# A scan's block ends multiplied up in three levels instead of six steps, and both reciprocal roots of a unit issued together

## The chip, the cores and the metric

One NeuronCore of a Trainium2 chip runs the whole program. The metric is the device time of one execution in microseconds (us), the median of several runs. The engines are TensorE (PE; its weight loads are listed as PEld), VectorE (DVE), ScalarE (ACT), GpSimd (POOL) and SyncE (SP, which here only issues DMAs). Each engine executes its own list of instructions in order; an instruction that waits holds up everything behind it on its engine.

## The reference

The program is a gated linear attention with a complex decay, then a dense layer, then a mixture of experts:

```python
mag = np.sqrt(a_re * a_re + a_im * a_im)
scale = np.minimum(mag, 0.999) / (mag + 1e-06)
a_re_n, a_im_n = (a_re * scale, a_im * scale)
for t in range(S):                      # state D x D per head, complex
    S = a_n[t] * S + k[t] v[t]^T        # complex product, row by row
    y[t] = q[t] . Re(S)
x = y                                   # 3072 tokens x 384
h = x @ w_in;  x = (h * np.cos(h)) @ w_out        # 384 -> 2048 -> 384
e = argmax(x @ w_gate); out = gate * sigmoid(x @ w_output_gate)[e] * (relu(x @ w1[e]) @ w2[e])
```

Shapes: 4 batches x 8 heads x 768 steps x 48 channels; 8 experts of 384 -> 1024 -> 384.

## The kernel before, in words

The 768 steps of a batch are cut into chunks of 128; two chunks make a unit, so there are twelve units. Within a chunk the recurrence becomes matrix products once the running products of the decay are known. These running products are the scan, and it is done with channels on the partitions: `a_t` holds the decays of a unit (real part, imaginary part and a third plane), `l_t` the running products, `qk_t` the queries and keys.

For each unit the scan has these parts:

- `squares`: the squares of both parts on ACT (L227, L228) and their sum on DVE into `nt[:, 1]`.
- `root` (L235): ACT takes the reciprocal square root of that sum into the third plane of `a_t` (L237).
- `normal`: scales the decays; it reads what `root` left, first with an ACT square (L269).
- `core` (L291): 64 positions of half a chunk are stored as 8 blocks of 8. First the eight positions in each block are multiplied up (seven complex steps, L296 to L301, 192 elements each). Then come the block ends: the product over all earlier blocks is needed for each block. This is the stretch that the change rewrites (L305 to L330). `lb[:, :, :, 7]` is the last position of each block; `pb[..., i]` is to become the product of the ends of blocks 0 to i-1; `nb` holds signed copies of the imaginary parts (minus and plus), so that one multiplication gives both cross terms of a complex product. Six steps i = 2 to 7 each issue two multiplications and an addition of 24 elements per partition. Then four multiplications of 672 elements spread `pb` over the blocks, and one addition of 1344 elements writes `l_t`.
- `inverse` (L239): ACT squares `l_t` (L244), DVE adds, ACT takes the reciprocal root (L248) and squares it (L249), and DVE finishes 1/|l|^2 and multiplies it into `qk_t`. For units 2 to 10 it is also given the next unit (`ua`), and calls `root` for it right after L249 in program order.
- `post`: two DVE multiplications into `qkt`, and DMAs that turn heads onto partitions (`qkr`).

Then `attn` of the unit makes its 256 columns of `x` on PE, and the dense layer follows in eight slots per unit: `mm1` (18 matmuls, L509), `act2` on ACT (a square whose sum is kept L517, a sine L518, a square L519), `act3` on DVE (L548), which also frees the PSUM buffer `h` (two buffers), and `mm2` (8 matmul records, L564). The reciprocal root and the sine are in different activation tables of ACT, so going from the one to the other issues an `ACT_TABLE_LOAD`.

While the slots of unit u run, `attn` of u+1 and the scan of u+2 are interleaved with them. In the first units the weights `w_in` and `w_out` are also decoded on DVE (L693 to L696), checked on ACT (L704, L705), turned on PE (L738, into an `h` buffer or an `o` buffer), copied by ACT (L739), multiplied with the gate weights on PE (L741) and copied once more (L742). The experts run from about 720 us on.

What stands where in each engine's list is decided when the program is built: a scheduler plays the instructions against a cost table with priorities, and writes each engine's list in the order it found. So a changed instruction can move others, on every engine.

Of the kernel before, what the change touches and what calls it, by code (L numbers as in the profile page):

```python
# [10 lines left out]
F32 = mybir.dt.float32  # L11
# [4 lines left out]
AF = mybir.ActivationFunctionType  # L16
# [27 lines left out]
NCOL = 3 * UC  # L44
# [91 lines left out]
def build(tc, ap, out, force=False):  # L136
    nc = tc.nc
    V, A, G, PE, SY = nc.vector, nc.scalar, nc.gpsimd, nc.tensor, nc.sync
    ctx = ExitStack()

    def pool(name, bufs=1, **kw):
        return tc.tile_pool(name=name, bufs=bufs, **kw)
# [16 lines left out]
    sp = scan_ctx.enter_context(pool("sp", 1, side="left"))  # L159
# [27 lines left out]
    a_t = sp.tile([128, 3, NCOL, C], F32, name="a_t")  # L187
    qk_t = sp.tile([128, 2, NCOL, C], F32, name="qk_t")
    l_t = sp.tile([128, 2, NCOL, C], F32, name="l_t")
    nt = sp.tile([128, 2, NCOL, C], F32, name="nt")  # L190
    qkt = sp.tile([128, 2, NCOL, 2, QP], F32, name="qkt")
    t12 = sp.tile([128, 2, 2, NCOL * 16], F32, name="t12")
    nb = sp.tile([128, 2, 2 * NCOL, 8], F32, name="nb")
    pb = sp.tile([128, 2, 2 * NCOL, 8], F32, name="pb")
    m0 = sp.tile([128, 3, NCOL], F32, name="m0")
    one = sp.tile([128, 2, NCOL], F32, name="one")
# [7 lines left out]
    def tt(e, o, a, b, op):  # L204
        return e.tensor_tensor(out=o, in0=a, in1=b, op=op)  # L205

    mark = {}

    def behind(ins, *names):

        for n in names:
            tc.add_manual_dep(ins.ins, mark[n].ins.name,
                              mybir.DependencyInfo(mybir.DependencyClass.NoSync, mybir.DependencyReason.DATA),
                              reason="issue order")

    MUL, ADD, SUB = ALU.mult, ALU.add, ALU.subtract


    def load_a(u):
        SY.dma_start(a_t[:, 0:2], ap["a"][u])  # L220
# [4 lines left out]
    def squares(u):  # L225

        A.activation(out=a_t[:, 2], in_=a_t[:, 0], func=AF.Square)  # L227
        A.activation(out=nt[:, 1], in_=a_t[:, 1], func=AF.Square)  # L228
        yield
        tt(V, nt[:, 1], a_t[:, 2], nt[:, 1], ADD)  # L230
        yield

    rooted = set()

    def root(u):  # L235
        rooted.add(u)
        A.activation(out=a_t[:, 2], in_=nt[:, 1], func=AF.Abs_reciprocal_sqrt)  # L237

    def inverse(u, ua):  # L239

        sq = qflat[:, 0:2 * N1].rearrange("p (r c t) -> p r c t", r=2, c=NCOL)
        y, q = (qflat[:, N1 * i:N1 * (i + 1)].rearrange("p (c t) -> p c t", c=NCOL) for i in (2, 3))
        r = nt[:, 0]
        A.activation(out=sq, in_=l_t, func=AF.Square)  # L244
        yield
        mark["add", u] = tt(V, r, sq[:, 0], sq[:, 1], ADD)
        yield
        A.activation(out=y, in_=r, func=AF.Abs_reciprocal_sqrt)  # L248
        A.activation(out=q, in_=y, func=AF.Square)  # L249
        if ua is not None:  # L250
            root(ua)
        yield
        tt(V, r, r, q, MUL)
        yield
        V.scalar_tensor_tensor(out=r, in0=r, scalar=2.0, in1=q, op0=SUB, op1=MUL)
        V.tensor_reduce(out=chk[:, 2 * u + 1:2 * u + 2], in_=r[:, :, 63:128:64], op=ADD, axis=AX.XY)
        yield
        for qk in range(2):
            h = slice(64 * qk, 64 * qk + 64)
            o = qk_t[:, qk, :, h]  # L260
            V.scalar_tensor_tensor(out=o, in0=o, scalar=-1.0, in1=r[:, :, h], op0=MUL, op1=MUL)
        yield
# [25 lines left out]
    lb = l_t.rearrange("p r c (h j b) -> p r (c h) j b", h=2, j=8)  # L288
    ab = a_t.rearrange("p r c (h j b) -> p r (c h) j b", h=2, j=8)

    def core(u):  # L291
        n = 2 * NCOL
        for j in range(1, 8):
            t1, t2 = (t12[:, i].rearrange("p r (c b) -> p r c b", b=8) for i in range(2))
            pr = ab[:, 0:2, :, 0] if j == 1 else lb[:, :, :, j - 1]
            tt(V, t1, pr, ab[:, 0:1, :, j].to_broadcast([128, 2, n, 8]), MUL)  # L296
            tt(V, t2, pr[:, ::-1], ab[:, 2:0:-1, :, j], MUL)
            if j == 1:
                A.copy(lb[:, :, :, 0], ab[:, 0:2, :, 0])
            yield  # L300
            tt(V, lb[:, :, :, j], t1, t2, ADD)  # L301
            yield
        if u + 1 < NU:
            load_a(u + 1)
        V.tensor_scalar(out=nb[:, 0], in0=lb[:, 1, :, 7], scalar1=-1.0, scalar2=None, op0=MUL)  # L305
        V.tensor_copy(nb[:, 1], lb[:, 1, :, 7])
        V.tensor_copy(pb[:, :, :, 1], lb[:, :, :, 7, 0])
        yield
        for i in range(2, 8):
            t1, t2 = t12[:, 0, :, 0:n], t12[:, 1, :, 0:n]  # L310
            tt(V, t1, pb[:, :, :, i - 1], lb[:, 0:1, :, 7, i - 1].to_broadcast([128, 2, n]), MUL)
            tt(V, t2, pb[:, ::-1, :, i - 1], nb[:, :, :, i - 1], MUL)
            yield
            tt(V, pb[:, :, :, i], t1, t2, ADD)
            yield
        V.tensor_scalar(out=nb[:, 0, :, 1:8], in0=pb[:, 1, :, 1:8], scalar1=-1.0, scalar2=None, op0=MUL)
        V.tensor_copy(nb[:, 1, :, 1:8], pb[:, 1, :, 1:8])
        yield
        k = 2 * n * 56
        t1, t2 = (qflat[:, k * i:k * (i + 1)].rearrange("p (r c j b) -> p r c j b", r=2, c=n, j=8) for i in range(2))  # L320
        bc = [128, n, 8, 7]
        for r in range(2):
            tt(V, t1[:, r], lb[:, r, :, :, 1:8], pb[:, 0, :, 1:8].unsqueeze(2).to_broadcast(bc), MUL)
            yield
            tt(V, t2[:, r], lb[:, 1 - r, :, :, 1:8], nb[:, r, :, 1:8].unsqueeze(2).to_broadcast(bc), MUL)
            yield
        sq = squares(u + 1) if u + 1 < NU else iter(())
        next(sq, None)
        la = l_t.rearrange("p r c (h j b) -> p (r c h) j b", h=2, j=8)[..., 1:8]
        tt(V, la, t1.rearrange("p r c j b -> p (r c) j b"), t2.rearrange("p r c j b -> p (r c) j b"), ADD)  # L330
        yield
        gates(u)
        yield
        run(sq)
        yield
# [57 lines left out]
    def scan(u):  # L393
        if u == 0:
            yield from squares(u)
            yield from normal(u)
        yield from core(u)
        more = 1 < u < NU - 1
        yield from inverse(u, u + 1 if more else None)
        yield from post(u)  # L400
        if more:
            yield from normal(u + 1)
# [353 lines left out]
    def run(g):  # L756
        for _ in g:
            pass
# [491 lines left out]
    if True:  # L1250
# [29 lines left out]
        with tc.high_priority(offset=100):  # L1280
            run(core(1))
            run(inverse(1, None))
        with tc.high_priority(offset=100):
            run(post(1))
        for u in range(NU):
# [26 lines left out]
            for s in range(NS):  # L1312
# [6 lines left out]
                i = u * NS + s - 2  # L1319
# [56 lines left out]
```

## Time and profile before

| | us |
|---|---|
| median of 3 runs | 973.82 (973.53 to 974.1) |
| the profiled execution, its own time | 972.88 |
| its span, first to last instruction | 971.1 |
| PE busy in the span | 894.8 (92%) |
| PEld busy | 756.5 (78%) |
| DVE busy | 664.3 (68%) |
| ACT busy | 582.0 (60%) |
| POOL busy | 134.3 (14%) |

The span is the time between the first and the last instruction of one profiled execution; 1.8 us of its own time lie around it. Busy shares are means over stages that differ: the weights and the first two scans up to about 104 us, the first units of the dense layer up to 180 us, the steady interleaving up to 640 us, and the last unit and the experts after that.

### The profile page before, as it was taken

How to read it: one execution, taken by the hardware profiler on the slowest of the kernel's cores; microseconds unless marked ns; L12 is line 12 of the kernel's file. 1: busy time of each engine (PE TensorE's matmuls, PEld its weight loads, DVE VectorE, ACT ScalarE, POOL GpSimd, SP SyncE). 2: the span in 40 equal slices, each digit the busy share in tenths (PEclk: the TensorE clock that was granted, in tenths of full speed). 3: DMA queues.
4: the chain of work that ended last, by engine and by line, in shares of the span. 5: the costliest groups of instructions: out<-in, count | busy, mean ns of one | idle time of the engine just before them, and what ended most of it. 6: DMA issues, size and time to landing. Idle time of an engine off the chain costs nothing.

```text
span 971.1 us, 16175 instructions
## 1 busy us (share of the span) xinstructions
PE 894.8 (92%) x5701; PEld 756.5 (78%) x5701; DVE 664.3 (68%) x1498; ACT 582.0 (60%) x1252; POOL 134.3 (14%) x246
## 2 busy tenths in 40 slices
PE   0566897999999999999999999999999999999997
PEld 0455685877777787777777778789899899999997
DVE  6989885887779786979698788445664553355521
ACT  6684866757574848585757665365773453355521
POOL 0010001002123002020312121101121110312111
PEclk9999999999999999999999999999999999999999
DMA  9813046345333223232333231440328532554100
GB/s 328 313 43 106 20 114 207 100 120 167 102 85 122 66 95 85 90 95 90 89 101 85 97 96 47 115 142 22 106 76 259 167 128 66 175 182 140 25 28 33
DMA packets 69789, 109.93 MB, mean 113 GB/s; under 512 B 14063, under 2 KB 51327, under 8 KB 69428
## 3 DMA queue, kind: packets, MB, share of 16 engines
q1 hardware_dynamic: 62724, 98.72, 32.9%
q0 software_dynamic: 6976, 10.10, 3.1%
q8 instruction: 47, 0.77, 0.3%
q14 instruction: 42, 0.34, 0.1%
HBM read 74.20 MB, written 21.86 MB: 99 GB/s over the span
## 4 chain that ended last, share of the span: by engine, by line
PE 50%; DVE 19%; ACT 11%; DMA 8%; issue 6%; SPq 4%; POOL 0%; DVEq 0%; another core or an unknown queue 0%; ACTq 0%; POOLq 0%
PE o L564 12%; PE h L952 10%; PE h L509 10%; PE p L976 6%; PE p L968 4%; DVE t L205 3%; DVE qkt L205 2%; DMA a_t<-in_a_dram 2%; PE sc L438 2%; DVE l_t L205 1%; DVE g L548 1%; DMA xs<-in_xz_dram 1%; DVE pt L205 1%; PE m L473 1%; DVE nt L205 1%
## 5 line engine op out<-in xcount | busy, mean ns | idle before, releaser
L509 PE MATMUL h<-x,wi 128*128 128x256 f32 x1728 | 247.7, 294 | 14.9 <-DMA x<-x 5.6
L564 PE MATMUL o<-wo,g 128*128 128x400 f32 x672 | 246.2, 506 | 0.0
L509 PEld LDWEIGHTS h<-x,wi 128*128 128x128 f32 x1728 | 218.9, 191 | 34.4 <-issue 8.7
L564 PEld LDWEIGHTS o<-wo,g 128*128 128x128 f32 x672 | 121.2, 192 | 72.2 <-issue 4.4
L952 PE MATMUL h<-xe,w1t 128*128 128x384 f32 (+6 forms) x576 | 118.7, 349 | 0.0
L956 DVE SCALAR_TENSOR_TENSOR hh<-h,hh 128x384 fp32r<-128x384 f32 (+6 forms) x64 | 37.2, 582 | 117.5 <-ACT hh L955 116.9
L952 PEld LDWEIGHTS h<-xe,w1t 128*128 128x128 f32 x576 | 101.8, 188 | 5.2
L517 ACT ACTIVATE g<-h 128x512 f32<-128x512 f32 x96 | 57.1, 594 | 79.6 <-PE h L509 75.7
L955 ACT ACTIVATE hh<-h 128x384 fp32r<-128x384 f32 (+6 forms) x64 | 32.8, 514 | 114.1 <-PE h L952 107.5
L548 DVE SCALAR_TENSOR_TENSOR g<-g,h 128x512 f32<-128x512 f32 x96 | 65.5, 682 | 43.5 <-ACT g L519 42.3
L572 POOL DMA_INDIRECT xs<-rows,si x46 | 55.7, 1211 | 172.0 <-ACT x L466 41.0
L976 PE MATMUL p<-w2t,hh 128*128 128x384 f32 (+1 forms) x384 | 76.7, 343 | 0.0
L976 PEld LDWEIGHTS p<-w2t,hh 128*128 128x128 f32 (+1 forms) x384 | 66.0, 186 | 1.5 <-DVE hh L956 0.3
L519 ACT ACTIVATE g<-g 128x512 f32<-128x512 f32 x96 | 60.8, 633 | 1.8
L438 PEld LDWEIGHTS sc<-qkr 96*128 96x128 f32 x384 | 51.5, 203 | 11.7 <-issue 3.5
L438 PE MATMUL sc<-qkr 96*128 96x128 f32 x384 | 57.0, 293 | 3.8 <-DMA qkr<-qkt 2.4
L518 ACT ACTIVATE g<-h 128x512 f32<-128x512 f32 x96 | 57.6, 600 | 1.8
L205 POOL TENSOR_TENSOR fg<-l_t,m 128x12 f32<-128x12 f32 x24 | 4.7, 215 | 373.5 <-DVE l_t L205 241.8
L572 POOL DMA_INDIRECT out_dram<-o,tok x28 | 34.6, 1234 | 149.6 <-issue 57.4
L968 PE MATMUL p<-hh,w2t 128*128 128x448 f32 (+2 forms) x216 | 47.6, 359 | 0.0
L205 DVE TENSOR_TENSOR t<-l_t,a_t 128x192 f32<-128x192 f32 x144 | 45.0, 352 | 1.4
L205 DVE TENSOR_TENSOR qkt<-l_t,qk_t 128x1536 f32<-128x1536 f32 (+1 forms) x26 | 41.2, 1630 | 0.3
(299 smaller groups left out, 1501.7 us busy)
## 6 DMA issues: line engine op xcount, KB each, us to landing
stg<-in_w_dram SPq DMA_DIRECT2D x32, 768.0 KB
qkr<-qkt SPq DMA_DIRECT2D x96, 146.2 KB
a_t<-in_a_dram SPq DMA_DIRECT2D x12, 768.0 KB
qk_t<-in_qk_dram SPq DMA_DIRECT2D x12, 768.0 KB
xs<-in_xz_dram SPq DMA_DIRECT2D x17, 401.0 KB
raw<-in_w_in_dram SPq DMA_DIRECT2D x7, 768.0 KB
raw<-in_w_out_dram SPq DMA_DIRECT2D x7, 768.0 KB
vt<-in_v_dram SPq DMA_DIRECT2D x24, 192.0 KB
```

The source lines that it names most:

```text
L205: return e.tensor_tensor(out=o, in0=a, in1=b, op=op)
L438: PE.matmul(sc[:, h], lhsT=t[:, h, 1, 0:C], rhs=t[:, h, 0, 0:C], start=True, stop=True)
L509: PE.matmul(h[:, i], lhsT=wis[s][:, wi, kk, i * 128:(i + 1) * 128], rhs=x_t[u][:, xi, kk], start=n == 0, stop=n == 8)
L517: A.activation(out=g, in_=h, func=AF.Square, accum_out=hck[:, u * NS + s:u * NS + s + 1])
L518: mark["sin"] = A.activation(out=g, in_=h, func=AF.Sin, scale=0.5)
L519: A.activation(out=g, in_=g, func=AF.Square, scale=float(np.sqrt(2.0)))
L548: V.scalar_tensor_tensor(out=g, in0=g, scalar=1.0, in1=hps.pop((u, s)), op0=SUB, op1=MUL)
L564: PE.matmul(o, lhsT=a[:, i, cs], rhs=w[:, i], start=s == 0 and n == 0 and i == 0, stop=s == NS - 1 and n == len(prods) - 1 and i == 1)
L572: sc = G.indirect_dma_start(in_offset=None, oob_is_err=False, **kw)
L952: PE.matmul(h, lhsT=w[:, wi, kk, f * 128:(f + 1) * 128], rhs=x[:, xi, kk], start=n == 0, stop=n == 8)
L968: PE.matmul(o2[e][d][:, 0:c], lhsT=w[:, wi, f, d * 128:(d + 1) * 128], rhs=hh[:, hi], start=f == 0 and n == 0, stop=f == KE - 1 and n == 2)
L976: mm = PE.matmul(o2[e][j][0:w_, 0:DM], lhsT=hh[:, hi, j * w_:(j + 1) * w_], rhs=w[:, wi, f], start=f == 0 and n == 0, stop=f == KE - 1 and ...
```

## The change

Three things are edited. (1) The block ends are multiplied up in three levels (distance 1, 2, 4) on all blocks at once, the second and third in place in `pb`. Each level multiplies once by the real and once by the imaginary part of the other factor, and then subtracts for the real and adds for the imaginary part. (2) `nb` and its four copies go; the spreading multiplications read the imaginary part from `pb`, and the last addition becomes a subtraction for the real part and an addition for the imaginary part, of 672 elements each. (3) When `inverse` calls `root` for the next unit, `root` must stand behind the square L249 on ACT in issue order.

```diff
-    def root(u):
+    def root(u, *after):
         rooted.add(u)
-        A.activation(out=a_t[:, 2], in_=nt[:, 1], func=AF.Abs_reciprocal_sqrt)
+        behind(A.activation(out=a_t[:, 2], in_=nt[:, 1], func=AF.Abs_reciprocal_sqrt), *after)
...
-        A.activation(out=q, in_=y, func=AF.Square)
+        mark["rs"] = A.activation(out=q, in_=y, func=AF.Square)
         if ua is not None:
-            root(ua)
+            root(ua, "rs")
...
-        V.tensor_scalar(out=nb[:, 0], in0=lb[:, 1, :, 7], scalar1=-1.0, scalar2=None, op0=MUL)
-        V.tensor_copy(nb[:, 1], lb[:, 1, :, 7])
-        V.tensor_copy(pb[:, :, :, 1], lb[:, :, :, 7, 0])
-        yield
-        for i in range(2, 8):
-            t1, t2 = t12[:, 0, :, 0:n], t12[:, 1, :, 0:n]
-            tt(V, t1, pb[:, :, :, i - 1], lb[:, 0:1, :, 7, i - 1].to_broadcast([128, 2, n]), MUL)
-            tt(V, t2, pb[:, ::-1, :, i - 1], nb[:, :, :, i - 1], MUL)
-            yield
-            tt(V, pb[:, :, :, i], t1, t2, ADD)
-            yield
-        V.tensor_scalar(out=nb[:, 0, :, 1:8], in0=pb[:, 1, :, 1:8], scalar1=-1.0, scalar2=None, op0=MUL)
-        V.tensor_copy(nb[:, 1, :, 1:8], pb[:, 1, :, 1:8])
-        yield
+        last = lb[:, :, :, 7]
+        V.tensor_copy(pb[:, :, :, 1], last[..., 0])
+        for d, a, b in ((1, last[..., 1:7], last[..., 0:6]), (2, pb[..., 3:8], pb[..., 1:6]), (4, pb[..., 5:8], pb[..., 1:4])):
+            t1, t2 = (t12[:, i].rearrange("p r (c b) -> p r c b", b=8)[..., 0:7 - d] for i in range(2))
+            bc = [128, 2, n, 7 - d]
+            tt(V, t1, a, b[:, 0:1].to_broadcast(bc), MUL)
+            tt(V, t2, a, b[:, 1:2].to_broadcast(bc), MUL)
+            yield
+            tt(V, pb[:, 0, :, d + 1:8], t1[:, 0], t2[:, 1], SUB)
+            tt(V, pb[:, 1, :, d + 1:8], t1[:, 1], t2[:, 0], ADD)
+            yield
...
-            tt(V, t2[:, r], lb[:, 1 - r, :, :, 1:8], nb[:, r, :, 1:8].unsqueeze(2).to_broadcast(bc), MUL)
+            tt(V, t2[:, r], lb[:, 1 - r, :, :, 1:8], pb[:, 1, :, 1:8].unsqueeze(2).to_broadcast(bc), MUL)
...
-        tt(V, la, t1.rearrange("p r c j b -> p (r c) j b"), t2.rearrange("p r c j b -> p (r c) j b"), ADD)
+        for r, op in ((0, SUB), (1, ADD)):
+            tt(V, lb[:, r, :, :, 1:8], t1[:, r], t2[:, r], op)
```

The changed program is a few lines shorter, so its line numbers in what follows are smaller: L244 becomes L243, L248 L247, L249 L248, L237 L236, L517 to L519 L513 to L515, L726 L722, L739 L735 and L742 L738.

The first place is VectorE's list at the block ends of unit 2. The kernel before (the first three of six steps):

```order
L305 TENSOR_SCALAR nb_130<-l_t_126 128x96
L306 COPY nb_130<-l_t_126 128x96
L307 COPY pb_131<-l_t_126 128x24
L205 TENSOR_TENSOR t12_129<-pb_131,l_t_126 128x2x12
L205 TENSOR_TENSOR t12_129<-pb_131,nb_130 128x2x12
L205 TENSOR_TENSOR pb_131<-t12_129 128x24
L205 TENSOR_TENSOR t12_129<-pb_131,l_t_126 128x2x12
L205 TENSOR_TENSOR t12_129<-pb_131,nb_130 128x2x12
L205 TENSOR_TENSOR pb_131<-t12_129 128x24
```

The changed kernel, all levels and the first instructions behind them (`x` is a column block of the attention's output, `nt` the sum in `squares`):

```order
L305 COPY pb_130<-l_t_126 128x24
L204 TENSOR_TENSOR t12_129<-l_t_126 128x24x6 x2
L204 TENSOR_TENSOR pb_130<-t12_129 128x12x6 x2
L204 TENSOR_TENSOR t12_129<-pb_130 128x24x5 x2
L204 TENSOR_TENSOR pb_130<-t12_129 128x12x5 x2
L204 TENSOR_TENSOR x_732<-pv_t_136,x_732 128x4x128
L204 TENSOR_TENSOR t12_129<-pb_130 128x24x3 x2
L204 TENSOR_TENSOR pb_130<-t12_129 128x12x3 x2
L204 TENSOR_TENSOR qkt_128<-l_t_126,pb_130 128x672 x4
L204 TENSOR_TENSOR nt_127<-a_t_124,nt_127 128x768
L204 TENSOR_TENSOR l_t_126<-qkt_128 128x96x7 x2
```

Twenty-three small instructions have become thirteen larger ones, and the addition of 1344 elements two of 672.

The second place is ScalarE's list in the first unit, around its square of `l_t` (`raw` and `wo` belong to the decoding of the weights). Before:

```order
L742 COPY raw_173<-o1_585 128x16
L726 COPY wo_594<-raw_173 128x2x16
L227 ACTIVATE a_t_124<-a_t_124 128x768
L228 ACTIVATE nt_127<-a_t_124 128x768
L726 COPY wo_620<-raw_295 128x2x384
L739 COPY raw_295<-o0_602 128x384
L739 COPY raw_295<-o1_611 128x384
L244 ACTIVATE qkt_128<-l_t_126 128x1536
L237 ACTIVATE a_t_124<-nt_127 128x768
```

After:

```order
L226 ACTIVATE a_t_124<-a_t_124 128x768
L227 ACTIVATE nt_127<-a_t_124 128x768
L738 COPY raw_172<-o1_575 128x16
L243 ACTIVATE qkt_128<-l_t_126 128x1536
L735 COPY raw_285<-o0_592 128x384
L722 COPY wo_584<-raw_172 128x2x16
L735 COPY raw_285<-o1_601 128x384
L236 ACTIVATE a_t_124<-nt_127 128x768
L722 COPY wo_610<-raw_285 128x2x384
```

The square of `l_t` moved ahead of three copies of 384 and 768 elements and a small one, and L227 ahead of the copy that waits for PE.

The third place is ScalarE's list in the inverse of unit 2, between the last two copies of the weights' decoding; `h_1338` and `h_1310` are the first `mm1` buffer of unit 1. Before (a table load stands directly ahead of the first row):

```order
L237 ACTIVATE a_t_124<-nt_127 128x768
L742 COPY rawr_303<-h_1228 128x16
L726 COPY wo_1246<-rawr_303 128x16
L739 COPY rawr_304<-h_1237 128x384
L244 ACTIVATE qkt_128<-l_t_126 128x1536
L517 ACTIVATE g_1384,hck_118<-h_1338 128x512
L518 ACT_TABLE_LOAD
L518 ACTIVATE g_1384<-h_1338 128x512
L248 ACT_TABLE_LOAD
L248 ACTIVATE qkt_128<-nt_127 128x768
L519 ACTIVATE g_1384<-g_1384 128x512
L742 COPY rawr_304<-h_1237 128x16
```

After (ahead of the first row stand L243, a table load, L247 and the 16-column copy L738):

```order
L248 ACTIVATE qkt_128<-qkt_128 128x768
L236 ACTIVATE a_t_124<-nt_127 128x768
L722 COPY wo_1228<-rawr_293 128x16
L735 COPY rawr_294<-h_1219 128x384
L513 ACTIVATE g_1356,hck_118<-h_1310 128x512
L354 COPY qkt_128<-fg_135 128x24
L355 COPY qkt_128<-fg_135 128x24
L514 ACT_TABLE_LOAD
L514 ACTIVATE g_1356<-h_1310 128x512
L515 ACTIVATE g_1356<-g_1356 128x512
L268 ACTIVATE nt_127,chk_116<-a_t_124 128x768
L738 COPY rawr_294<-h_1219 128x16
```

The two roots now stand together behind one table load, and the copies of the weights' decoding moved behind them. Over the part of the list that is executed, the table loads go from 42 to 28.

## Rows read from the trace of the kernel before

**Rows 1.** Windows by stage: us, each engine's busy time (instructions), granted clock, DMA.

```profile
0.00:104.00 104.00, 50.38 (x250) 43.53 (x250) 88.70 (x183) 67.89 (x146) 3.18 (x17) 1.00 0.55 189
104.00:180.00 76.00, 68.67 (x430) 54.11 (x431) 57.65 (x109) 54.91 (x122) 5.84 (x26) 0.93 0.35 108
180.00:640.00 460.00, 450.99 (x3055) 352.66 (x3055) 359.55 (x834) 296.48 (x636) 75.42 (x153) 1.00 0.34 98
640.00:971.10 331.10, 324.78 (x1968) 306.17 (x1966) 158.41 (x374) 162.69 (x351) 49.86 (x50) 1.00 0.35 112
```

**Rows 2.** Waits of PE, 180 to 640 us: total us, times, longest.

```profile
PE sc L438 <- DMA qkr<-qkt: 2.2, 2, 1.4
PE pv_t L462 <- DVE tp L205: 1.6, 2, 1.3
PE h L509 <- DVE g L548: 1.3, 2, 0.7
```

**Rows 3.** DVE groups by shape: busy us, mean ns of one | idle before.

```profile
L205 DVE TENSOR_TENSOR t<-l_t,a_t 128x192 f32<-128x192 f32 x144 | 45.0, 352 | 1.4
...
L205 DVE TENSOR_TENSOR l_t<-qkt 128x1344 f32<-128x1344 f32 x12 | 18.6, 1550 | 0.0
```

**Rows 4.** Timeline of DVE, block ends of unit 1: start, us [idle before].

```profile
94.32 0.21 DVE L305 TENSOR_SCALAR nb<-l_t 128x96 f32<-128x96 f32 x1
...
97.71 0.20 DVE L205 TENSOR_TENSOR t<-pb,l_t 128x24 f32<-128x24 f32 x1
97.83 0.20 DVE L205 TENSOR_TENSOR t<-pb,nb 128x24 f32<-128x24 f32 x1
98.06 0.20 DVE L205 TENSOR_TENSOR pb<-t 128x24 f32<-128x24 f32 x1
...
98.53 1.62 DVE L205 TENSOR_TENSOR qkt<-l_t,pb 128x672 f32<-128x672 f32 x2
...
103.94 0.69 DVE L548 SCALAR_TENSOR_TENSOR g<-g,h 128x512 f32<-128x512 f32 x1 [1.38 <-ACT g L519]
```

**Rows 5.** Timeline of ACT, first unit, up to the square of l_t.

```profile
48.73 0.18 ACT L742 COPY raw<-o 128x16 f32<-128x16 f32 x1 [0.77 <-PE o L741]
...
50.54 0.87 ACT L726 COPY wo<-raw 128x768 f32<-128x768 f32 x1
51.32 0.87 ACT L739 COPY raw<-o 128x384 f32<-128x384 f32 x2
52.08 1.48 ACT L244 ACTIVATE qkt<-l_t 128x1536 f32<-128x1536 f32 x1
```

**Rows 6.** Timeline of DVE, first unit, the sum of those squares.

```profile
53.59 0.96 DVE L205 TENSOR_TENSOR nt<-qkt 128x768 f32<-128x768 f32 x1 [1.97 <-ACT qkt L244]
```

**Rows 7.** Timeline of PE, first transposes, and two later stalls.

```profile
63.64 0.90 PE L423 MATMUL m<-ident,qkt 128*128 128x128 f32 x3 [4.05 <-DVE qkt L205]
...
116.84 2.39 PE L509 MATMUL h<-x,wi 128*128 128x256 f32 x18 [0.66 <-DVE g L548]
...
170.25 4.74 PE L509 MATMUL h<-x,wi 128*128 128x256 f32 x25 [3.47 <-ACT rawr L742]
```

**Rows 8.** Timeline of DVE, 113 to 118 us: decoding of weights around one act3.

```profile
116.11 0.68 DVE L548 SCALAR_TENSOR_TENSOR g<-g,h 128x512 f32<-128x512 f32 x1
116.71 0.95 DVE L696 SCALAR_TENSOR_TENSOR raw<-raw 128x768 uint32<-128x768 uint32 x1
```

**Rows 9.** Timeline of ACT, inverse of unit 2.

```profile
158.66 1.28 ACT L237 ACT_TABLE_LOAD   x1
...
167.48 1.28 ACT L248 ACT_TABLE_LOAD   x1
168.77 0.84 ACT L248 ACTIVATE qkt<-nt 128x768 f32<-128x768 f32 x1
...
170.04 0.15 ACT L742 COPY rawr<-h 128x16 f32<-128x16 f32 x1
```

**Rows 10.** Window behind that stall: us, busy by engine, granted clock (third last).

```profile
170.20:173.00 2.80, 2.75 (x15) 2.75 (x16) 2.61 (x4) 0.83 (x2) 0.88 (x1) 0.61 0.01 3
```

More of the change, by code (lines that the diff above doesn't have):

```diff
@@ L192, in build @@
     t12 = sp.tile([128, 2, 2, NCOL * 16], F32, name="t12")
-    nb = sp.tile([128, 2, 2 * NCOL, 8], F32, name="nb")
     pb = sp.tile([128, 2, 2 * NCOL, 8], F32, name="pb")
@@ L328, in core @@
         next(sq, None)
-        la = l_t.rearrange("p r c (h j b) -> p (r c h) j b", h=2, j=8)[..., 1:8]
-        tt(V, la, t1.rearrange("p r c j b -> p (r c) j b"), t2.rearrange("p r c j b -> p (r c) j b"), ADD)
+        for r, op in ((0, SUB), (1, ADD)):
+            tt(V, lb[:, r, :, :, 1:8], t1[:, r], t2[:, r], op)
         yield
```

## The prediction

> **What bounds the kernel now.** I read the windows by stage first [rows 1]. Up to 104 us no engine is full, but DVE is busy for 88.7 us of it and ACT for 67.9, while PE works half the time: here the weights' decoding and the first two scans pass from engine to engine. From 104 to 180 us PE has 68.7 of 76.0 us. From 180 to 640 us PE is busy for 451.0 of 460.0 us, DVE for 359.6 (78%), ACT for 296.5 (64%). After 640 us PE has 324.8 of 331.1 us, and nothing that is changed runs there: the scan of the last unit is over. So the place decides what a saved microsecond is worth. In the head it may count in full. In the steady stage at most the 9.0 us in which PE is idle can come back, and the waits of PE say who owes them: the three largest are the DMA of the turned heads (2.2 us), DVE's `tp` (1.6) and `act3` (1.3) [rows 2]. All of these stand behind the scan's work in DVE's or ACT's list.
>
> A short stall costs PE more than its length. Behind the longest one after 104 us, 3.47 us long [rows 7], the granted clock is 0.61 over 2.8 us [rows 10], that is, mostly the lower level of 1.2 GHz, and the 25 matmuls there take 4.74 us [rows 7].
>
> **Part 1, the block ends.** In unit 1 they stand with nothing between them: from 94.32 to 98.53 us, so 4.21 us before the spreading begins [rows 4]. Two multiplications that don't depend on each other start 0.12 us apart, one that needs its predecessor 0.23 us behind it [rows 4]. The new shapes of 144, 120, 72, 60 and 36 elements aren't in the trace; they lie between 24 elements (0.20 us) [rows 4] and 192 (0.352 us) [rows 3], so about 0.9 ns for an element. A level is then two multiplications, a dependent subtraction and an addition. The first one costs 0.12 + 0.11 (120 elements more than 24, at 0.9 ns) for the first multiplication, 0.23 + 0.11 for the second, whose result is waited for, and 0.16 and 0.27 for the two of 72 elements: 1.00 us. In the same way 0.92 for the second and 0.79 for the third; with the one copy left, 0.1 to 0.2 us, it is about 2.85 us. The bounds are twelve instructions at 0.12 (1.4 us) and twelve at 0.352 (4.2 us). I take 2.85, as the sizes are nearer to 24 than to 192 in the last levels and in between in the first. The addition of 1344 elements (1.55 us) [rows 3] becomes two of 672, of which a pair of multiplications takes 1.62 us [rows 4]: 0.07 more. So DVE saves 4.21 - 2.85 - 0.07 = 1.3 us a unit, 15.5 us in all; by the bounds 0 to 2.7 us a unit.
>
> Next comes what is late instead. After the block ends of unit 1 DVE sits idle for 1.38 us until ACT's second square [rows 4]; in the first unit it waits 1.97 us for ACT's square of `l_t` [rows 6]. So in both, DVE's saving alone only lengthens a wait for ACT. I cost it at nothing there; ACT's own list is the cover, and where that list gets shorter, DVE's saving is what lets it be used. That the tile `nb` goes shifts other tiles in memory; no row shows that an address costs anything, so nothing for it.
>
> **Part 2, the head.** In ACT's list of the first unit the square of `l_t` now stands ahead of a copy of 768 elements and two of 384 (50.54 to 52.08 us, 1.5 us) and a small one (0.1), and L227 and L228 fill the 0.77 us in which ACT waited for PE [rows 5]. So ACT could start it at about 49.7 instead of 52.08. DVE writes `l_t` 1.3 us earlier, by about 48.5, and is no longer in the way. The copies that were passed over now stand between this square and the two of `inverse`, but DVE has six decode instructions of up to 0.95 us [rows 8] between its sum at 53.59 [rows 6] and the multiplication that needs them, which hides that. From there DVE is in one piece up to `post`, and PE's first transposes wait 4.05 us for it [rows 7]. I take -2.3 us, all on the path, since the DMAs of the turned heads and the first slot follow from it one by one. Bounds: 0 (the decoding of weights takes the time back) and -3.
>
> In the third slot of the first unit there is a small loss. DVE's list had one decode instruction behind an `act3` (116.71 behind 116.11) [rows 8], which now stands ahead of it; that `act3` is the one that PE waits for at 116.84, 0.66 us [rows 7]. One decode starts 0.87 us before its successor: +0.8.
>
> **Part 3, the roots.** Fourteen table loads fewer at 1.28 us [rows 9] are 18.0 us of ACT's time, of which 1.3 to 2.6 us fall in each unit from 2 on. The one PE stall that hangs directly on them is that of 3.47 us [rows 7]: PE waits for the last 16-column copy at 170.04, and on ACT this stands behind two table loads and both roots, 11.4 us after 158.66 [rows 9]. Before, three loads lie in that stretch (root, sine, root again); in the new list one lies in the shadow of DVE's sum and one in the open, so about two go (2.6 us). The square L268 comes into it (0.84, as L248 [rows 9]). It is shorter by about 1.7, but the copy still stands last, so I don't expect the stall to go: -1.2 us, between 0 and -5 (the stall and what the low clock costs behind it).
>
> The Trainium skill, "ScalarE: Activation LUTs", section What ACT_TABLE_LOAD costs, gives about 1283 ns for the load and 1380 ns more of drain, 2.66 us for a switch. The trace has the 1283 ns, but the next instruction starts 0.01 us behind the load's end (167.48 + 1.28, and 168.77) [rows 9], so no drain is seen. By the page fourteen loads would free 37 us of ACT; by the rows it is 18.0, and I use the rows.
>
> **Part 4, the steady stage.** There each of ten units frees 1.3 us on DVE and about 1.8 us on ACT, while PE waits 0.9 us a unit (9.0 in all). Most of these waits name an instruction that stood behind the scan's work, so more than half could go; but PE's list changes order too, and new waits come with it. I take -4.0, between 0 and -8.
>
> **Sum.** -2.3 + 0.8 - 1.2 - 4.0 = -6.7 us. The profiled execution took 972.88 us (span 971.1), so 966.2; the median of the runs shown stands 0.94 us above it, so 967.1.
>
> **Rivals.**
> 1. DVE, not PE, is the bound of the interleaved stages. For it: from 0 to 104 us DVE is the busiest engine [rows 1], PE's records are pipelined, so that a busy PE may be a slow one, and PEld is busy for only 352.7 of 460 us. Against it: DVE is idle for 100 us of the steady stage. It would give back the 1.3 us of twelve units, and 1 more in the first with its moved copies: 973.8 - 15.5 - 1 = 957. A rule of the Trainium skill, "Perfetto Trace Analysis", section Identifying the Most-Contended Engine, speaks for this rival: headroom of TensorE is to be read from the share of weight loads, not of matmuls, and that is 77% here against DVE's 78%. By that rule DVE would come first; the rows on PE's idle time name too little waiting for it.
> 2. Nothing comes through. PE is full in the steady stage, the head is paced by SP's DMAs and by the decoding, and what DVE and ACT save lengthens their waits. For it: both waits of DVE right after the block ends. Against it: PE's transposes do wait for DVE in the head. It gives 973.8, less 0 to 1.5: 973.
> 3. Slower. With the next unit's root behind the inverse, ACT runs load, L247, L248 and L236 as one block: 1.28 + 0.84 + 0.84 + 0.84 = 3.8 us, and waits in it for DVE's sum of 0.96 us. PE has two `h` buffers, and a slot of PE is 18 + 8 matmul records. From the point where this block, with that wait, outlasts a slot of about 5 us (2.39 us for the 18 [rows 7], and somewhat more for the 8), the next slot's squares come late in nine units. If each then costs a stall like the 0.66 us at 116.84 [rows 7], it is +5.9; with the +0.8 and half of the head that leaves +5.5: about 979. Against it: the block held two loads before, and the sine between them.
> 4. The change doesn't do what it says: if the scheduler parted the roots in most units, the loads would stay. ACT's list shows 28, so only one unit still has three loads; this rival is out, and gets no chance.
>
> **How the numbers follow.** My forecast has 0.62, with its own range of 962 to 971.5; rival 1 0.10, rival 2 0.17, rival 3 0.11. For this kernel 0.2%, some 2 us, is about what a measurement can tell from no change: faster below 971.9, slower above 975.8. Rivals 1 and most of the forecast are faster, 0.71; rival 2 and the rest 0.17; rival 3 0.12. The range reaches from 959.5 to 975, which leaves out rivals 1 and 3, 0.2 in all.
>
> **What would show it.** Right: DVE's block ends take 2.5 to 3.2 us; ACT's square of `l_t` in the first unit starts near 50, PE's first transposes near 61.5, and what follows them some 2 us earlier; table loads are 28; PE's idle time from 180 to 640 us is about 5 us. The stall at 170 is still there, near 2 us long. Wrong: PE's first transposes still at 63 us (then the head gave nothing), or PE idle as long as before in the steady stage with other names behind the waits (rival 2), or `mm1` waiting for `act3` in unit after unit (rival 3).

## The result, and the profile after

The changed kernel takes 965.0 us (median of 5 runs, 963.7 to 967.99) against 973.82 for the kernel before (5 runs, 972.28 to 974.1): a ratio of 0.9914, with a 95% interval of 0.9895 to 0.9933. The prediction was 967.1 us, with a range of 959.5 to 975. The profiled execution took 965.0 us, 963.2 of it span, against 972.88 and 971.1.

This window of the kernel after answers to the third row of [rows 1], with the same columns.

```profile
180.00:640.00 460.00, 455.94 (x3124) 359.55 (x3123) 354.14 (x757) 283.70 (x616) 68.84 (x153) 1.00 0.35 101
```

PE is idle for 460.0 - 455.9 = 4.1 us there, against 9.0, and gets 3124 matmul records done in it, against 3055. The waits of PE in that stage, which answer to [rows 2]:

```profile
PE sc L434 <- DMA qkr<-qkt: 2.1, 1, 2.1
PE pv_t L458 <- DVE tp L204: 1.4, 1, 1.4
PE pv_t L453 <- DVE pt L204: 0.6, 2, 0.3
```

These are nearly all that is left; the wait for `act3` is gone from the list.

VectorE's block ends of unit 1, which answer to [rows 4]:

```profile
92.75 0.19 DVE L305 COPY pb<-l_t 128x24 f32<-128x24 f32 x1
92.85 0.53 DVE L204 TENSOR_TENSOR t<-l_t 128x144 f32<-128x144 f32 x2
...
95.37 3.16 DVE L204 TENSOR_TENSOR qkt<-l_t,pb 128x672 f32<-128x672 f32 x4
99.60 0.96 DVE L204 TENSOR_TENSOR nt<-a_t,nt 128x768 f32<-128x768 f32 x1 [1.07 <-ACT nt L227]
```

They take 95.37 - 92.75 = 2.62 us, against 4.21. But the row at 99.60 shows VectorE idle behind the spreading, for ScalarE's second square of the next unit's decays. What those squares wait for is where the experiments end up.

Around unit 0 and unit 2 these rows answer to [rows 5], [rows 7] and [rows 9]. The timelines of ACT, DVE and PE (`raw` and `rawr` belong to the decoding of the weights):

```profile
50.12 1.51 ACT L243 ACTIVATE qkt<-l_t 128x1536 f32<-128x1536 f32 x1
...
153.70 0.84 ACT L226 ACTIVATE a_t<-a_t 128x768 f32<-128x768 f32 x1 [3.62 <-DMA a_t<-in_a_dram]
...
155.75 0.16 ACT L738 COPY raw<-h 128x16 f32<-128x16 f32 x1
...
168.72 0.15 ACT L738 COPY rawr<-h 128x16 f32<-128x16 f32 x1
```

```profile
81.97 0.68 DVE L204 TENSOR_TENSOR pt<-sc,cb 128x512 f32<-128x512 f32 x1
82.57 0.68 DVE L204 TENSOR_TENSOR x<-pv_t,x 128x512 fp32r<-128x512 f32 x1
```

```profile
61.97 0.90 PE L419 MATMUL m<-ident,qkt 128*128 128x128 f32 x3 [1.14 <-DVE qkt L204]
...
92.29 0.76 PE L505 MATMUL h<-x,wi 128*128 128x256 f32 x2 [5.29 <-DMA x<-x]
...
116.38 1.33 PE L505 MATMUL h<-x,wi 128*128 128x256 f32 x9 [1.39 <-DVE g L544]
...
155.97 0.92 PE L734 MATMUL h<-ident,rawr 128*128 128x128 f32 x3 [3.61 <-ACT raw L738]
...
168.93 3.58 PE L505 MATMUL h<-x,wi 128*128 128x256 f32 x18 [2.52 <-ACT rawr L738]
```

The square of `l_t` starts 2.0 us earlier, PE's first transposes 1.67 us, the first `mm1` only 0.93 us. The wait at 116 grew from 0.66 to 1.39 us, and the one at 169 shrank from 3.47 to 2.52. The wait at 156 grew too; in the kernel before it is this row of PE:

```profile
156.20 0.63 PE L738 MATMUL h<-ident,rawr 128*128 128x128 f32 x3 [2.20 <-ACT raw L742]
```

The copy that PE waits for there, at 155.75 on ScalarE, stands behind the square at 153.70, and that square waited 3.62 us for the load of the decays.

To compare kernels I use one stretch with the same work in each: from 104 us to the first evacuation of unit 9's output on ScalarE, in which every kernel has 3472 to 3488 matmul records on PE. Kernel before, then after (window, its length, busy time of PE; the rest of the row is not needed):

```profile
104.00:639.70 535.70, 519.36 (x3484) 406.60 (x3485) 416.90 (x943) 351.09 (x756) 81.26 (x179) 0.99 0.34 99
```

```profile
104.00:631.28 527.28, 515.65 (x3482) 406.10 (x3482) 407.42 (x851) 333.81 (x740) 72.35 (x169) 0.99 0.34 101
```

So unit 9 is evacuated 8.4 us earlier. PE's idle time falls from 16.3 to 11.6 us, and its busy time for the same work from 519.4 to 515.7: the gain is idle time and, nearly as much, faster matmuls.

### The profile page after: what moved, and what is told of

Same layout as the page of the kernel before. It is cut to its first block, busy times and chain, and to the rows that moved or that the text cites. A ratio compares the mean times of both kernels' runs of the same rounds, so it can differ in the third digit from the quotient of the medians.

```text
span 963.2 us, 16039 instructions
## 1 busy us (share of the span) xinstructions
PE 891.7 (93%) x5701; PEld 756.2 (79%) x5701; DVE 655.0 (68%) x1390; ACT 565.8 (59%) x1238; POOL 127.1 (13%) x246
## 4 chain that ended last, share of the span: by engine, by line
PE 66%; ACT 10%; DVE 8%; DMA 6%; issue 5%; SPq 4%; POOL 1%; DVEq 0%; ACTq 0%; POOLq 0%
PE o L560 19%; PE h L505 15%; PE h L948 10%; PE p L972 6%; PE p L964 4%; PE sc L434 3%; PE m L469 2%; PE pv_t L453 2%; DMA a_t<-in_a_dram 2%; PE pv_t L458 2%; SPq L365 1%; DVE t L204 1%; SPq L368 1%; DVE qkt L204 1%; DVE l_t L204 1%
## 5 line engine op out<-in xcount | busy, mean ns | idle before, releaser
L505 PE MATMUL h<-x,wi 128*128 128x256 f32 x1728 | 244.2, 293 | 13.4 <-DMA x<-x 6.2
L513 ACT ACTIVATE g<-h 128x512 f32<-128x512 f32 x96 | 57.2, 595 | 100.7 <-PE h L505 99.8
L568 POOL DMA_INDIRECT xs<-rows,si x46 | 51.3, 1114 | 249.6 <-ACT x L462 64.1
L515 ACT ACTIVATE g<-g 128x512 f32<-128x512 f32 x96 | 60.8, 634 | 2.0
```

The lines of the kernel that those rows point to most:

```text
L505: PE.matmul(h[:, i], lhsT=wis[s][:, wi, kk, i * 128:(i + 1) * 128], rhs=x_t[u][:, xi, kk], start=n == 0, stop=n == 8)
L513: A.activation(out=g, in_=h, func=AF.Square, accum_out=hck[:, u * NS + s:u * NS + s + 1])
L515: A.activation(out=g, in_=g, func=AF.Square, scale=float(np.sqrt(2.0)))
L568: sc = G.indirect_dma_start(in_offset=None, oob_is_err=False, **kw)
```

## Experiments

All runs with times. "Loads" are the table loads that ScalarE executes, "wait" is ScalarE's idle time in front of the first square of the next unit's decays (`a_t`) between 104 and 650 us, nine units in all; "idle" and "busy" are PE's in the stretch just told. These three are those of the profiled execution. The ratios are to runs of the kernel before on the same chip (medians 972.2 to 973.8 us).

| kernel | block ends | loads | time, us | ratio to before | wait | idle | busy |
|---|---|---|---|---|---|---|---|
| e4 | levels | 44 | 985.8 | 1.0143 [1.0122, 1.0164] | 33.9 | 24.6 | 521.1 |
| e12 (list of e1) | levels | 42 | 979.1 | 1.0061 [1.0041, 1.0080] | 36.5 | 25.4 | 518.9 |
| e1 | levels | 42 | 978.3 | 1.0058 [1.0038, 1.0078] | 32.4 | 18.9 | 518.4 |
| before | six steps | 42 | 973.8 | 1 | 25.7 | 16.3 | 519.4 |
| e5 | six steps | 38 | 967.1 | 0.9949 [0.9931, 0.9967] | 26.5 | 13.2 | 515.7 |
| e2 | six steps | 30 | 968.5 | 0.9965 [0.9947, 0.9983] | 20.0 | 12.7 | 518.5 |
| after | levels | 28 | 965.0 | 0.9914 [0.9895, 0.9933] | 32.1 | 11.6 | 515.7 |
| e11 (list of after) | levels | 28 | 964.0 | 0.9908 [0.9891, 0.9925] | 30.1 | 12.5 | 515.0 |
| e9 | six steps | 26 | 964.3 | 0.9906 [0.9887, 0.9926] | 26.3 | 11.1 | 516.1 |
| e8 | levels | 26 | 961.6 | 0.9872 [0.9849, 0.9894] | 34.1 | 9.6 | 514.7 |
| w9c | six steps | 26 | 958.7 | 0.9850 [0.9823, 0.9876] | 2.7 | 6.4 | 514.3 |
| w8b | levels | 26 | 958.3 | 0.9839 [0.9813, 0.9865] | 19.4 | 8.0 | 514.7 |
| w5c | levels | 28 | 954.4 | 0.9805 [0.9777, 0.9833] | 1.5 | 7.3 | 511.2 |
| w8c | levels | 28 | 954.1 | 0.9797 [0.9772, 0.9822] | 2.7 | 6.2 | 510.3 |

The profile puts most of this wait to the load (a DMA) and some of it to instructions of VectorE. In the kernel before, then after (total, times, longest):

```profile
ACT a_t L227 <- DMA a_t<-in_a_dram: 21.9, 7, 4.3
ACT a_t L227 <- DVE pb L205: 3.0, 1, 3.0
ACT a_t L227 <- DVE nb L316: 0.8, 1, 0.8
```

```profile
ACT a_t L226 <- DMA a_t<-in_a_dram: 27.5, 8, 5.8
ACT a_t L226 <- DVE mx L598: 4.6, 1, 4.6
```

The square needs nothing of `pb`, `nb` or `mx`. In the trace the last landing of the load stands at most 0.4 us ahead of the square's start in all of these waits, so they are one wait, and the column adds the lines up.

**The levels alone (e1).** The kernel after, without the hold on the root.

```diff
-            root(ua, "rs")
+            root(ua)
```

> The changed kernel with its three levels, but the next unit's root is not held behind the inverse: 42 executed table loads instead of 28, and lists on PE and DVE that hardly differ from the changed kernel's. Theory A (both parts free PE from waiting in the steady stage, the loads through ACT's list): about 3 us above the changed kernel, 967 to 970, with PE idle 6 to 8 us from 180 to 640 us. Theory B (VectorE's shorter list gives it all): 964 to 966. Theory C (the loads give it all): 972 to 974.

Measured: 978.3 us, slower than before. No theory had that. VectorE's work is shorter as in the kernel after, yet PE's idle time in the common stretch is 18.9 us, more than the kernel before has. The waits of PE from 180 to 650 us:

```profile
PE pv_t L453 <- DVE pt L204: 5.4, 3, 2.2
PE pv_t L458 <- DVE tp L204: 2.9, 2, 1.7
```

The longest of them, seen in the timeline of all engines (rows of the other instructions left out):

```profile
427.11 0.84 ACT L226 ACTIVATE a_t<-a_t 128x768 f32<-128x768 f32 x1 [3.50 <-DMA a_t<-in_a_dram]
427.86 0.83 ACT L227 ACTIVATE nt<-a_t 128x768 f32<-128x768 f32 x1
428.59 0.61 ACT L515 ACTIVATE g<-g 128x512 f32<-128x512 f32 x1
...
429.71 1.28 ACT L236 ACT_TABLE_LOAD   x1
...
432.93 1.28 ACT L514 ACT_TABLE_LOAD   x1
...
434.85 0.63 ACT L515 ACTIVATE g<-g 128x512 f32<-128x512 f32 x1
...
435.51 0.69 DVE L544 SCALAR_TENSOR_TENSOR g<-g,h 128x512 f32<-128x512 f32 x1 [1.56 <-ACT g L515]
...
436.59 0.68 DVE L204 TENSOR_TENSOR pt<-sc,cb 128x512 f32<-128x512 f32 x1
...
437.33 0.43 PE L453 MATMUL pv_t<-pt,vt 128*48 128x128 f32 x4 [2.20 <-DVE pt L204]
```

Read it from the end: PE waits for `pt`, which stands on VectorE behind `act3`; `act3` waits for ScalarE's square L515 at 434.85; and that square is late because ScalarE lost 3.50 us to the load of the decays and then 2 x 1.28 us to the table of the root, there and back. The square of the slot before, L515 at 428.59, had been queued behind L226 and L227 all that time.

**The roots alone (e2).** The six steps as before, the root held behind the inverse's square.

```diff
-            root(ua)
+            root(ua, "rs")
```

> The kernel before with its six steps and signed copies, but the next unit's root held behind the inverse: 30 executed table loads instead of 42, VectorE's work unchanged. Theory A: 969 to 972. Theory B: 973 to 975. Theory C: 964 to 967.

Measured: 968.5 us, a gain of 0.35%, on 30 loads. It lies just below the range of Theory A and above that of C. The parts don't add: levels +0.6%, roots -0.35%, both -0.9%. But this edit also moved other rows: some 960 of the 5701 in TensorE's list stand elsewhere than before, so it is not the roots' worth alone. Between e1 and the kernel after only some 180 do.

**Two repeats (e11, e12).** A further place for other work inside each level, with and without the hold.

```diff
             tt(V, t1, a, b[:, 0:1].to_broadcast(bc), MUL)
+            yield
             tt(V, t2, a, b[:, 1:2].to_broadcast(bc), MUL)
```

> The kernel after with one more place in each level of the block ends at which other work may be listed between the two products: same operations and the same 28 executed loads, other lists on all engines. Theory 1 (loads decide): 964 to 967. Theory 2 (order decides): off 965 by 2 us or more, 959 to 972.

> As the run e11_levels_other_order, without holding the reciprocal square root behind the inverse's square: 42 executed loads in place of 28. Theory 1: e11 + 14 x 1.28 = e11 + 18 us. Theory 2: within 5 us of e11 in either direction. Theory 3 (hidden until TensorE waits): e11 + 4 to 13, as the kernel with levels alone stood 13 us above the kernel after.

The scheduler put nothing there: the lists are, row for row, those of the kernel after and of e1. So both are repeats, not the other orders that I meant to test. As such they are useful: 964.0 beside 965.0, and 979.1 beside 978.3. The hold is worth 13 to 15 us where the block ends are levels, between what Theory 3 and Theory 1 said.

**The price of a table load (e4, e5, e9).** In e4 a sine of one element on ScalarE stands between the two roots, so that their tables are loaded apart again; the other lists differ from those of the kernel after in a dozen rows each at most.

```diff
+            mark["sn"] = behind(A.activation(out=spare, in_=one[:, 1, 0:1], func=AF.Sin), "rs")
-            root(ua, "rs")
+            root(ua, "sn")
```

> The changed kernel with a sine of one element between the square behind the first root and the second root of units 2 to 10, which adds two table loads of 1.28 us to most of these units (44 executed instead of 28, some 20 us of ScalarE) and leaves the lists of all other engines as they are, but for a few rows. Theory A: 3 to 5 us above the changed kernel, 968 to 970. Theory B: within 1 us of it, 964 to 966. Theory C: 972 or more.

Measured: 985.8 us, 20.8 more than after by the medians and 22.3 by the ratios, for 16 loads more (20.5 us at 1.28) and nine small sines: ScalarE's added time came through in full. That is inside Theory C's open range; A and B are out. The profiled executions differ by 18.0 us. In the common stretch it is 18.4, of which 13.0 are idle time of PE (24.6 against 11.6), and 5.4 slower matmuls (521.1 against 515.7).

In e5 three copies of the kernel before are written in the opposite order; e9 is e5 with the root held.

```diff
-        V.tensor_scalar(out=nb[:, 0], in0=lb[:, 1, :, 7], scalar1=-1.0, scalar2=None, op0=MUL)
-        V.tensor_copy(nb[:, 1], lb[:, 1, :, 7])
         V.tensor_copy(pb[:, :, :, 1], lb[:, :, :, 7, 0])
+        V.tensor_copy(nb[:, 1], lb[:, 1, :, 7])
+        V.tensor_scalar(out=nb[:, 0], in0=lb[:, 1, :, 7], scalar1=-1.0, scalar2=None, op0=MUL)
```

> The kernel before with its three copies at the block ends written in the opposite order: the same work to the instruction, but the scheduler's lists come out in another order on all engines. Theory A (the work that is saved counts): within 1.5 us of the kernel before, 972.3 to 975.3. Theory D (the order that the scheduler happens on makes the difference, and the gain is one draw of it): outside of that by 3 us or more, to either side.

> Block ends as before the change (six steps, signed copies, the three copies in the opposite order as in the run with 967.07 us), and the reciprocal square root of the next unit held behind the inverse's square: 26 executed table loads on ScalarE in place of 38, nearly the same lists of TensorE and VectorE otherwise. Theory 1 (a table load costs the kernel about its full 1.28 us): 967.1 - 12 x 1.28 = 951.7, cut off at about 956, since TensorE waits only some 12 us in all between 104 and 650 there. Theory 2 (the order of the lists decides, the loads are mostly hidden): 963 to 972 with no tie to the number of loads. Theory 3 (a load costs only while TensorE waits are left in the steady stage, which are 5.5 us there): 962 to 965.

e5 took 967.1 us, 0.5% less than before. That looked like the order alone, as Theory D has it, but its list also lost four table loads (38 for 42); how much is due to which was not separated. e9 took 964.3 us: twelve loads fewer than e5 gave only 2.8 us by the medians and 4.2 by the ratios, 0.2 to 0.35 us for each. So Theory 1 of that run (full price) is refuted for the six steps, and Theory 3 fits; Theory 2 could have this time too, but not the 15 us between e11 and e12, whose other lists are much alike. With the levels the same loads cost 1.0 us each (e1 and e12) to 1.4 us (e4). I read this as a matter of ScalarE's slack, of which more is gone with the levels; no run varies the slack alone.

**Where the slack went.** With 26 loads and six steps e9 takes the same time as the kernel after and its repeat with levels and 28 loads (964.3, and 965.0 and 964.0). There the levels' 1.5 us a unit on VectorE bring nothing. This led to Theory W: what VectorE saves comes out as ScalarE's wait for the decays. I took the figures for it from the lines that name the DMA, 27.5 us in the kernel after and 10 to 15 in e2 and e9. That was a misreading, since in those two more of the wait stands under other names. For e9:

```profile
ACT a_t L227 <- DMA a_t<-in_a_dram: 15.3, 5, 4.3
ACT a_t L227 <- DVE pb L205: 7.1, 2, 4.4
ACT a_t L227 <- DVE pt L205: 2.2, 1, 2.2
ACT a_t L227 <- DVE t L205: 1.7, 1, 1.7
```

Added up, it is 20.0 to 26.5 us in the four kernels with six steps and the squares where they were, and 30.1 to 36.5 in the six with levels. So the levels do lengthen the wait, but by 6 to 12 us, and most of it was there before.

The load of the next unit's decays overwrites `a_t`, so it can't start before the scan's last product has read it. In the kernel after, that pair of products starts at 417.94 on VectorE and the square at 423.01 on ScalarE, after a wait:

```profile
417.94 0.63 DVE L204 TENSOR_TENSOR t<-l_t,a_t 128x192 f32<-128x192 f32 x2
...
419.06 0.19 DVE L305 COPY pb<-l_t 128x24 f32<-128x24 f32 x1
...
423.01 0.85 ACT L226 ACTIVATE a_t<-a_t 128x768 f32<-128x768 f32 x1 [1.34 <-DMA a_t<-in_a_dram]
```

That is 423.01 - 418.57 = 4.4 us for the load. In other units SyncE issues it later, up to 7.0 us behind the product (unit 11), so its list adds to the wait. In units 2 to 9 the block ends, with what is listed among them, take 4.7 to 7.5 us with the six steps and 2.6 to 3.6 with the levels. The squares are written behind the spreading that follows; with the levels that comes sooner, and the rest of the load is waited for with the `act2` of the slots (their gates) queued behind. To test it, the squares are listed later.

**One wait of unit 2 taken out first (e8).** The squares of unit 2 go behind the first slot's gate (its `act2`), and its root behind the inverse's square.

```diff
+            root(u, *(["rs"] if u == 2 else []))
-        sq = squares(u + 1) if u + 1 < NU else iter(())
+        sq = squares(u + 1) if u + 1 < NU and u != 1 else iter(())
-                gs = chain((normal(2), scan(2)))
+                gs = chain((iter((None,)), squares(2, "g0"), normal(2), scan(2)))
```

> The kernel after, with unit 2's squares issued behind the first slot's gate and its reciprocal square root held behind the inverse's square: 26 executed loads in place of 28, and ScalarE no longer waits for unit 2's decays ahead of the first slot's gate. Theory 1: 965.0 - 2 x 1.28 - about 2 of TensorE's wait at 103.5 = 960.5 (959 to 962). Theory 2: anywhere within 5 us of 965, the wait at 103.5 gone or not. Theory 3: 962 to 964.

Measured: 961.6 us, 3.4 below the kernel after, inside the ranges of Theories 1 and 2 and 0.4 below that of Theory 3, so it doesn't part them. The wait of `mm1` for `act3` between 96 and 110 us fell from 3.2 to 2.2 us, but 2.2 us for a DMA of `x` came beside it. Unit 0 is evacuated at 167.8 us in place of 174.2, of which 3.0 us are left at unit 9, and the wait for the decays in the other units stayed (34.1 us).

**The squares late (w5c), and the same with the six steps (w9c).** Only the issue order of two ScalarE instructions in units 3 to 11 is asked for, and the work is the same, but the scheduler's other lists change with it: some 900 of TensorE's 5701 rows stand elsewhere in w5c than in the kernel after, and some 630 in w9c than in e9.

```diff
         for r, op in ((0, SUB), (1, ADD)):
-            tt(V, lb[:, r, :, :, 1:8], t1[:, r], t2[:, r], op)
+            mark["la"] = tt(V, lb[:, r, :, :, 1:8], t1[:, r], t2[:, r], op)
+        if 1 < u < NU - 1:
+            behind(mark["s0", u + 1], "la")
+            behind(mark["s1", u + 1], "la")
```

> The kernel after, with ScalarE's two squares of the next unit's decays listed behind the last sum of the scan (VectorE) in place of ahead of it: same work, 28 executed loads as in the kernel after. Theory W (what the levels save on VectorE came out as ScalarE's wait for the load of the decays, 27.5 us between 104 and 650 in the kernel after, 10 to 15 us in the kernels with the six steps and the roots in one trip): that wait falls under 10 us, and the time to 959 to 963. Rival S (that wait is slack of ScalarE and costs nothing): 963 to 967, whatever the wait.

> The kernel of the run with 964.25 us (six steps, copies in the opposite order, roots in one trip, 26 executed loads) with the same late squares, still 26 loads. Theory W: there is less of the wait to remove (15.3 us), so less is won: 962 to 965, and the kernel with the levels and late squares is at least 1.5 us faster. Rival S: 962 to 967 and within 1.5 us of it.

Measured: 954.4 us for w5c, 10.6 below the kernel after, and 958.7 for w9c, 5.6 below e9. Both are better than Theory W's own ranges, and outside those of Rival S. In w5c this is left of the 32.1 us of ScalarE's wait:

```profile
ACT a_t L226 <- DVE qkt L204: 1.1, 2, 0.7
ACT a_t L226 <- DMA a_t<-in_a_dram: 0.4, 1, 0.4
```

The common stretch of w5c:

```profile
104.00:622.44 518.44, 511.18 (x3484) 402.21 (x3485) 405.95 (x851) 332.34 (x741) 85.45 (x172) 1.00 0.35 102
```

Against the kernel before w5c saves 17.3 us in this stretch, 9.1 of idle time and 8.2 of busy time. And with the wait gone the levels are worth something: w5c is 4.3 us below w9c, although it has two loads more.

Where this is won says more than the sum. From 104 us to the first evacuation of unit 0, the kernel after, then w5c:

```profile
104.00:174.15 70.15, 62.58 (x403) 50.02 (x403) 54.51 (x97) 49.97 (x116) 3.51 (x16) 0.93 0.40 122
```

```profile
104.00:168.09 64.09, 59.46 (x413) 47.72 (x414) 50.88 (x94) 49.04 (x114) 4.65 (x19) 1.00 0.39 122
```

Of the 8.8 us by which w5c is ahead of the kernel after at unit 9, 6.1 are won here, where only one of the nine waits lies, that of 3.62 us at 153.70. In w5c the copy that PE waits for stands ahead of the squares, and the squares don't wait. The timelines of ACT and PE:

```profile
152.82 0.17 ACT L743 COPY raw<-h 128x16 f32<-128x16 f32 x1
...
155.34 0.85 ACT L226 ACTIVATE a_t<-a_t 128x768 f32<-128x768 f32 x1
```

```profile
153.04 0.63 PE L739 MATMUL h<-ident,rawr 128*128 128x128 f32 x3 [0.32 <-ACT raw L743]
```

PE waits 0.32 us there and not 3.61. Two stalls of 0.76 and 0.54 us, at 158 and 163, come in place of that of 2.52 us at 169, and the granted clock of the stretch is 1.00 and not 0.93. The other eight waits, 28.5 us of them, lie behind, and what lies between the evacuations of units 0 and 9 is shorter by only 2.8 us. In w9c, too, 4.2 of the 6.5 us at unit 9 are won before unit 0's evacuation, but in part by a stall at 118 that lies ahead of all late squares (2.30 us in e9, 0.75 in w9c), so by the order of the lists.

**Both together (w8c, w8b).** The late squares in e8, once behind the last sum as in w5c, once one sum earlier.

```diff
-            behind(mark["s0", u + 1], "la")
-            behind(mark["s1", u + 1], "la")
+            behind(mark["s0", u + 1], "sp")
+            behind(mark["s1", u + 1], "sp")
```

> The kernel of the run with 961.59 us (no wait of ScalarE for unit 2's decays ahead of the first gate) with the late squares: 28 executed loads in place of 26. Theory W: 956 to 960. Rival S: 961 to 964, since two loads come back and nothing is won.

> As w8c_no_wait_unit2_late, but the squares behind the last spreading product, one sum earlier: 26 executed loads. Theory W: between 957 and 961, with a wait for the decays between that of the kernel before it (30.7 us) and that of w8c. Rival S: 961 to 963.

Measured: 954.1 us for w8c, below Theory W's range, and 958.3 for w8b, inside it. With e8 that makes three sizes of the wait: 34.1 us and 961.6, 19.4 us and 958.3, 2.7 us and 954.1, on average 0.24 us for each microsecond of ScalarE's wait (7.5 us for 31.4). From e8 to w8b only some 55 rows of TensorE's list change, from e8 to w8c some 440. It is an average and not a price, as the places where w5c won its time show. w8c is not distinguishable from w5c; no gain of the edit for unit 2 is to be seen once the squares are late. Both stand some 2% below the kernel before (the intervals reach from 1.7 to 2.3%).

## Why the prediction was right, step by step

| step | predicted, us | measured, us |
|---|---|---|
| block ends of a unit | 2.85 | 2.62 |
| head, at the first `mm1` | -2.3 | -0.9 |
| third slot, decode ahead of `act3` | +0.8 | +0.7 |
| stall at 170 | -1.2 | -0.95 |
| right behind that stall, up to unit 0's evacuation | 0 | -1.3 |
| steady stage, unit 0's to unit 9's evacuation | -4.0 | -5.8 |
| after it | 0 | +0.5 |
| in other places, with +1.4 at the stall of 156 | 0 | -0.2 |
| profiled execution | -6.7 | -7.9 |

*Part 1* holds: the durations built from 24 and 192 elements came out 0.2 us too long. "Costed at nothing" was right beyond the two units for which I said it, and with the cover that I named, ScalarE's list: between 104 and 650 us VectorE's waits for the square L227 (L228 before) grew from 4.7 to 10.0 us. What I did not ask is what those squares wait for.

*The head* failed in one sentence: that all else follows "one by one". It did up to PE's transposes (-1.67). Then VectorE's list has `pt` at 81.97 ahead of `x` at 82.57, which stood first before (83.54, with `pt` at 84.14); `x` is only 0.97 us earlier, and its DMA and the first `mm1` with it.

*The stall at 170* behaved as the prediction worked it out from ScalarE's list. Behind it the granted clock is as low as in [rows 10] (0.61 from 168.9 to 172.5 us), and 18 matmuls take 3.58 us. The sum's -6.7 came near the -7.9 partly by luck: what the head gave too little, 1.4 us, came back as 1.3 us behind this stall, for which the sum had no term of its own.

*Part 3* had the loads at 28 and 18.0 us of ScalarE, right, but credited only the one stall directly and put the rest into Part 4. The runs with and without the hold put the loads at 13 to 15 us where the block ends are levels. Nothing in the trace of before showed that: with the six steps twelve loads fewer were worth some 3 to 4 us (e9 against e5, and e2 against before). The Trainium skill, "ScalarE: Activation LUTs", section What ACT_TABLE_LOAD costs, has 1380 ns of drain beside each load; the run with 16 more loads puts the whole at 20.8 / 16 = 1.3 us, or 1.4 by the ratios, so here too no more than about the load is seen.

*Part 4* is the step that failed in its reasoning, though its sum came close (-5.8 against -4.0). It let each part free PE by itself. The levels alone make this stage 5.9 us longer (e1 against before); they shorten the time in which the load of the decays is hidden. That the longer wait is all of it is not shown, as the levels alone were not run with late squares. The ceiling, "at most the 9.0 us in which PE is idle can come back", held in this stage: even in w5c it is only 8.6 us shorter than before, 6.4 of idle and 2.2 of busy time. What the sum had too little of lies ahead of this stage, from 104 us to unit 0's evacuation. There w5c wins 8.7 us on the kernel before, 2.7 of idle time and 6.0 of busy time, at a granted clock of 1.00 against 0.93. The prediction said itself that a stall costs more than its length, and allowed up to -5 for the one at 170, but took -1.2.

*The rivals.* Rival 1 (VectorE bounds) is refuted by the levels alone: less work on it, and a longer time. The rule in the Trainium skill ("Perfetto Trace Analysis", section Identifying the Most-Contended Engine), by which the share of weight loads put VectorE first, is not borne out by that run. Rival 2 is out by the time. Rival 3 didn't come in the changed kernel, where no wait of PE for `act3` is left in the steady stage; but e1 and e4 show its kind, a slot's squares late behind the scan's work on ScalarE, and they are slower than before.

*Left open:* how much of e5's gain is its order and how much its four loads; what the levels alone would give with late squares, which was not run; and how much of the other differences is the order of the lists. Every edit but those of e4 and e11 moves many other rows, and e5, with the work of the kernel before and four loads fewer, moved the time by 0.5%. So the direction of what the late squares give rests on four comparisons (3.3 to 10.6 us), and the place at 153 us shows how; their sizes are not the wait's alone.

## What to carry to other kernels

When a saving shortens the stretch between a transfer's start and its first use, ask what hid the transfer: here it was in part the work that was saved, and some of the gain came out as a wait in another engine's list, ahead of work that PE needs. Add a wait up over all the names that the profile gives it before comparing kernels by it. Take the parts of a change apart by runs even where the sum is as forecast, since a part that harms can hide behind one that helps. In a queue that issues in order, an instruction that waits for a DMA belongs behind what the busiest engine waits for: moving two of them, with the reordering that came along, was worth more than the whole change. And most of that was won at one place, so ask of each wait what stands behind it, and not only how long it is.

## What the runs showed of the hardware

For the same work (3472 to 3488 records) PE's busy time runs from 510.3 us, with 6.2 us of idle time (w8c), to 521.1 us, with 24.6 (e4); the granted clock over this stretch is 1.00 in w8c and 0.98 in e4. The two go together only roughly (e12 has 25.4 us of idle time and 518.9 of busy time), but idle time alone understates what a wait costs. A table load took 1.28 us wherever it stood, and cost the kernel between 0.2 us and 1.4 us.
